# Second expert layer in seven block products instead of eight (Strassen form, chained in PSUM)

## The chip, the cores and the metric

The kernel runs on one core of one Trainium2 chip. The metric is the device time of one execution in microseconds (us); lower is better. Every kernel here was run several times beside the kernel before on the same chip. Engines are named as in the profile: PE is TensorE's matmul, PEld its weight load, DVE is VectorE, ACT is ScalarE, POOL is GpSimd.

## The reference, cut to what matters

A linear attention gives 4608 tokens of 512 values (left out). They then go through eight experts, each with two layers, whose results are weighted by a routing matrix and added.

```python
def _moe_ref(x, w_gate, w1, w2):        # x 4608 x 512, 8 experts, hidden width 1024
    ...                                 # P (4608 x 8) by eight rounds of normalising
    out = np.zeros((N, D), dtype=np.float32)
    for e in range(E):
        h = np.maximum(x @ w1[e], 0.0)  # first layer:  512 -> 1024
        ye = h @ w2[e]                  # second layer: 1024 -> 512
        out += P[:, e:e + 1] * ye
    return out.astype(np.float32)
```

## The kernel before

A small planner in the kernel (`_Plan`) takes every piece of work with its engine, an assumed duration, its dependences, its buffers and a priority, and settles the program order of each engine before anything runs. On the chip each engine works its list in that order.

The work of the experts is cut into units: one expert and one group of 512 tokens, 8 x 9 = 72 units. A unit has eight first-layer blocks (four matmuls of 512 columns each, then a relu on ScalarE that writes h in fp16) and 32 second-layer matmuls of 512 columns (four token tiles by eight pieces of the hidden width). VectorE then takes each token tile out of PSUM, the memory in which the matmuls leave their sums (this is called an eviction below), multiplies it by the routing weight and adds it to the accumulator.

```python
def unit(e, g):
    ...
    for f in range(NFT):                                   # eight first-layer blocks
        def f_hq(_, f=f, ghq=ghq, use_att=use_att):
            ...
            for c in range(NDT):
                nc.tensor.matmul(ghq["tile"], lhsT=gw1["tile"][:, c, ts(f, P)], rhs=xT[c][:, ds(512 * g, 512)],
                                 start=(c == 0), stop=(c == NDT - 1))
        def f_rl(_, ghq=ghq, gh=gh):
            gh["tile"] = hpool.tile([P, 512], FP16, tag="h", name="h")
            nc.scalar.activation(out=gh["tile"], in_=ghq["tile"], func=AF.Relu)
    ...
    for half in range(2):                                  # second layer: 2 x 4 x 4 matmuls of 512 columns
        for tt in range(4):
            def f_y(_, half=half, tt=tt):
                ...
                for f in range(4 * half, 4 * half + 4):
                    nc.tensor.matmul(gy[tt]["tile"], lhsT=hs[f]["tile"][:, ds(P * tt, P)], rhs=gw2["tile"][:, f, :],
                                     start=(f == 0), stop=(f == NFT - 1))
    ...
    for tt in range(4):                                    # eviction, experts 1 to 7
        nc.vector.scalar_tensor_tensor(out=acc[g][:, tt, :], in0=gy[tt]["tile"],
                                       scalar=P_sb[:, gg, e:e + 1], in1=acc[g][:, tt, :],
                                       op0=ALU.mult, op1=ALU.add)
```

Expert 0 is special: it runs beside the attention, before the routing weights are known, so its tiles are copied out and scaled later.

The softmax here doesn't subtract the row's maximum and nothing guards it: scores larger than these inputs give would overflow.

Of the kernel before, what the change touches and what calls it, by code (L numbers as in the profile page):

```python
# [9 lines left out]
FP32 = mybir.dt.float32  # L10
FP16 = mybir.dt.float16
# [102 lines left out]
def kernel(  # L114
# [10 lines left out]
    nc = tc.nc  # L125
# [20 lines left out]
    wpool = ctx.enter_context(tc.tile_pool(name="wpool", bufs=2))  # L146
    hpool = ctx.enter_context(tc.tile_pool(name="hpool", bufs=12))
    yps = ctx.enter_context(tc.tile_pool(name="yps", bufs=1, space=PSUM))
# [21 lines left out]
    p_vv, p_kvz, p_qpT, p_xn, p_rden = (S_.pool(2) for _ in range(5))  # L170
    p_att, p_hq, p_h = S_.pool(2), S_.pool(2), S_.pool(12)
    p_w1, p_w2 = S_.pool(2), S_.pool(2)
# [262 lines left out]
    def f_close(_):  # L435
        front.close()
        accp.append(ctx.enter_context(tc.tile_pool(name="accp", bufs=1)))
        for g in range(NA, NG):
            acc[g] = accp[0].tile([P, 4, 512], FP32, tag=f"acc{g}", name=f"acc{g}")
    t_close = add(("none", 0.0), f_close, deps=front_ids, prio=0.0)  # L440

# [4 lines left out]

    def unit(e, g):
        gw1, tw1, gw2, tw2 = w_t[e]
# [3 lines left out]
        th = []  # L452
        hs = []
        for f in range(NFT):
            use_att = e > 0 and f % 2 == 1
            ghq = S_.grp(p_att if use_att else p_hq)
            gh = S_.grp(p_h)

# [5 lines left out]

            def f_rl(_, ghq=ghq, gh=gh):
                gh["tile"] = hpool.tile([P, 512], FP16, tag="h", name="h")
                nc.scalar.activation(out=gh["tile"], in_=ghq["tile"], func=AF.Relu)  # L467
            t1 = add(("pe", 0.87), f_hq, deps=[tw1, prev_hq[0]] + xd, acq=[ghq], use=[gw1], prio=ui + 0.1 * f + 0.35)
            prev_hq[0] = t1
            th.append(add(("act", 0.6), f_rl, deps=[t1], acq=[gh], use=[ghq], prio=ui - 400.0))  # L470
            hs.append(gh)
        gy = [S_.grp(p_ye[tt]) for tt in range(4)]
        ty = [None] * 4
        for half in range(2):
            for tt in range(4):
                def f_y(_, half=half, tt=tt):
                    if half == 0:
                        gy[tt]["tile"] = yps.tile([P, 512], FP32, tag=f"ye{tt}", name=f"ye{tt}")
                    for f in range(4 * half, 4 * half + 4):
                        nc.tensor.matmul(gy[tt]["tile"], lhsT=hs[f]["tile"][:, ds(P * tt, P)], rhs=gw2["tile"][:, f, :],  # L480
                                         start=(f == 0), stop=(f == NFT - 1))
                ty[tt] = add(("pe", 0.87), f_y, deps=[tw2, ty[tt]] + th[4 * half:4 * half + 4],
                             acq=[gy[tt]] if half == 0 else [], use=[gw2] + hs[4 * half:4 * half + 4],
                             prio=ui + 0.1 * (4 * half + tt) + 0.3)
        for tt in range(4):
            gg = 4 * g + tt

            def f_fin(eng, tt=tt, gg=gg):
                if e == 0:
                    copy(eng, acc[g][:, tt, :], gy[tt]["tile"])  # L490
                else:
                    nc.vector.scalar_tensor_tensor(out=acc[g][:, tt, :], in0=gy[tt]["tile"],  # L492
                                                   scalar=P_sb[:, gg, e:e + 1], in1=acc[g][:, tt, :],
                                                   op0=ALU.mult, op1=ALU.add)
            tf = add({"act": 0.65, "dve": 0.69} if e == 0 else ("dve", 0.75), f_fin,
                     deps=[ty[tt], fin_prev.get(gg), p_done if e > 0 else None,
                           t_close if e == 0 and g >= NA else None], use=[gy[tt]], prio=ui - 400.0)
            if e == 0:
                def f_s(_, tt=tt, gg=gg):
                    nc.vector.tensor_scalar(out=acc[g][:, tt, :], in0=acc[g][:, tt, :],  # L500
                                            scalar1=P_sb[:, gg, 0:1], scalar2=None, op0=ALU.mult)
                tf = add(("dve", 0.35), f_s, deps=[tf, p_done], prio=50.0 + gg)
            fin_prev[gg] = tf
            if e == E - 1:
                def f_o(_, tt=tt, gg=gg):
                    for half in range(2):
                        bb, j = divmod(2 * gg + half, NJ)
                        dst = AP(tensor=out.tensor, offset=(S * bb + j) * DM, ap=[[NJ * DM, PW], [1, DM]])
                        nc.sync.dma_start(out=dst, in_=acc[g][64 * half:64 * half + 64, tt, :])
                add(("sp", 1.0), f_o, deps=[tf], prio=0.0)  # L510

    w_t[1] = load_w1(1, prio=0.0, after=60.0) + load_w2(1, prio=0.0, after=70.0)
    for e in range(E):
        if e >= 2:
            w_t[e] = load_w1(e, prio=float(e), deps=[w_t[e - 1][1]]) + load_w2(e, prio=float(e), deps=[w_t[e - 1][3]])
        for g in range(NG):
            unit(e, g)
    S_.run()
# [30 lines left out]
```

## Time and profile before

| | before |
|---|---|
| time, median of 4 runs | 1100.96 us |
| profiled run: span, granted TensorE clock | 1099.9 us, 0.991 |
| from the first matmul after expert 0 to the end of the last matmul's slot (its start plus the pace) | 869.65 us |
| steady unit (nine in a row take 124.32 us) | 13.813 us |
| one matmul of 512 columns, start to start (13.813 us / 64) | 215.8 ns |

In the timeline a line has the start in us, the time from the first start to the last end, the engine, the source line, the operation, what it writes and reads, the shape, how many instructions the line joins, and in brackets how long the engine had been idle and what ended that. The tile hq is a first-layer block, ye a second-layer sum in PSUM. TensorE is pipelined: the ends shown are modelled and overlap the next start. So I read its pace from starts alone. A group of eight matmuls that starts 0.87 us before the next group costs 0.87 us, even where the line says 1.04. A wait of TensorE is then the distance of two starts less the number of matmuls times their pace.

The prediction shows the steady part. The end of the kernel looks like this in the timeline before; it is needed later:

```profile
1090.18 3.89 PE L480 MATMUL ye<-w,h 128*128 128x512 f16 x16
...
1091.09 2.49 PEld L480 LDWEIGHTS <-h 128*128 128x128 f16 x13 [0.59 <-ACT h L467]
...
1093.70 0.38 PE L480 MATMUL ye<-w,h 128*128 128x512 f16 x1
```

The last unit has no next unit to put between its layers, so the last sixteen matmuls wait once for the last relu: the last of them (the third line, the end of the same group, from a narrower window) starts at 1093.70 instead of 1090.18 + 15 x 0.2158 = 1093.42, 0.28 us late, and its slot ends at 1093.91.

### The profile page before, as it was taken

The numbers are of one execution on the slowest core, as the hardware profiler recorded it, in microseconds if no ns is written. First come the engines' busy times: TensorE is split into PE (matmuls) and PEld (weight loads), VectorE is DVE, ScalarE is ACT, GpSimd is POOL, SyncE is SP. The second block draws the span as 40 slices with busy tenths as digits, with TensorE's granted clock in tenths as the row PEclk, the third lists the DMA queues.
The fourth block names the chain that finished last, engine by engine and source line by source line (L and its number), as shares of the span: only waits on it lengthen the run. The fifth ranks groups of instructions, "written<-read, shape, count | busy, mean of one in ns | idle before, by whom it ended". The sixth has DMA issues, their size and how long they took to land.

```text
span 1099.9 us, 13561 instructions
## 1 busy us (share of the span) xinstructions
PE 1060.9 (96%) x5536; PEld 504.3 (46%) x5536; DVE 355.9 (32%) x597; ACT 431.8 (39%) x693; POOL 54.8 (5%) x55
## 2 busy tenths in 40 slices
PE   3799999999999999999999999999999999999997
PEld 2455564444444444444444444444444444444443
DVE  7877866712222222222222222222222222222222
ACT  4677653443333333333333333333333333333332
POOL 3423110000000000000000000000000000000000
PEclk9799999999999999999999999999999999999999
DMA  9878400040004000040003000040003100013333
GB/s 276 320 198 249 144 1 1 1 77 1 1 1 70 8 1 1 1 77 1 1 1 63 15 1 1 1 77 1 1 1 54 24 1 1 1 39 77 77 77 77
DMA packets 31951, 55.41 MB, mean 50 GB/s; under 512 B 2704, under 2 KB 10896, under 8 KB 31888
## 3 DMA queue, kind: packets, MB, share of 16 engines
q1 hardware_dynamic: 18816, 37.76, 11.4%
q0 software_dynamic: 13072, 16.79, 9.6%
q8 instruction: 43, 0.70, 0.3%
q14 instruction: 20, 0.16, 0.0%
HBM read 61.88 MB, written 9.44 MB: 65 GB/s over the span
## 4 chain that ended last, share of the span: by engine, by line
PE 90%; DVE 6%; DMA 2%; ACT 1%; issue 0%; POOL 0%; SPq 0%; DVEq 0%; POOLq 0%; ACTq 0%
PE hq L462 44%; PE ye L480 43%; DMA vin<-in_v_dram 1%; PE kv_ps L260 1%; DMA kin<-in_k_dram 1%; DVE tk L238 1%; DVE xn L328 1%; DVE tq L238 1%; PE xt_ps L339 1%; PE qt_ps L285 1%; PE num_ps L323 0%; DVE ek L236 0%; DVE kvz L194 0%; DVE eq L236 0%; PE lg_ps L356 0%
## 5 line engine op out<-in xcount | busy, mean ns | idle before, releaser
L467 ACT ACTIVATE h<-hq 128x512 f16<-128x512 f32 x576 | 343.3, 597 | 604.5 <-PE hq L462 604.3
L462 PE MATMUL hq<-xT,w 128*128 128x512 f16 x2304 | 525.3, 379 | 0.6 <-ACT h L467 0.6
L480 PE MATMUL ye<-w,h 128*128 128x512 f16 x2304 | 525.6, 380 | 0.1
L492 DVE SCALAR_TENSOR_TENSOR acc<-ye,P_sb,acc 128x512 f32<-128x512 f32 x252 | 189.2, 751 | 679.8 <-PE ye L480 658.6
L480 PEld LDWEIGHTS <-h 128*128 128x128 f16 x2304 | 224.2, 98 | 265.9 <-issue 2.4
L462 PEld LDWEIGHTS <-w 128*128 128x128 f16 x2304 | 223.7, 98 | 263.1 <-issue 1.8
L180 POOL DMA_DIRECT2D w<-in_moe_w_dram x16 | 13.2, 828 | 694.7 <-PE hq L462 672.5
L196 POOL CAST vv<-vin 64x1152 f16<-64x1152 f32 x32 | 40.3, 1258 | 97.4 <-PE kv_ps L260 43.9
L285 PE MATMUL qt_ps<-ident,tq 128*128 128x128 f16 x144 | 13.4, 232 | 15.6 <-DVE tq L238 11.0
L260 PE MATMUL kv_ps<-vv,tk 128*128 128x260 f16 x144 | 22.1, 306 | 5.7 <-DVE qpT L194 4.1
L328 DVE TENSOR_TENSOR xn<-num_ps,rden 128x512 f16<-128x512 f32 (+1 forms) x48 | 26.5, 595 | 2.7 <-PE num_ps L323 1.9
L323 PE MATMUL num_ps<-kvz,qpT 128*128 128x128 f16 x160 | 16.2, 229 | 9.6 <-DVE xn L328 7.5
L225 ACT ACTIVATE ek<-kin 128x1152 f16<-128x1152 f32 x16 | 18.6, 1162 | 13.7 <-DMA kin<-in_k_dram 9.8
L225 ACT ACTIVATE eq<-qin 128x1152 f16<-128x1152 f32 x16 | 18.5, 1158 | 8.7 <-DVE tq L238 6.4
L192 ACT COPY acc<-ye 128x512 f32<-128x512 f32 x29 | 16.9, 584 | 10.0 <-PE ye L480 10.0
L323 PEld LDWEIGHTS <-qpT 128*128 128x128 f16 x160 | 12.3, 101 | 18.2 <-issue 12.5
L260 PEld LDWEIGHTS <-tk 128*128 128x128 f16 x144 | 14.7, 107 | 11.7 <-DVE qpT L194 4.7
L285 PEld LDWEIGHTS <-tq 128*128 128x128 f16 x144 | 10.6, 104 | 19.3 <-DVE tq L238 11.0
L238 DVE TENSOR_TENSOR tk<-tk,ek 128x1152 f16<-128x1152 f16 x16 | 17.7, 1107 | 1.1
L500 DVE TENSOR_SCALAR acc<-acc,P_sb 128x512 f32<-128x512 f32 x36 | 15.0, 490 | 9.1 <-ACT acc L192 9.1
L233 ACT ACTIVATE tk<-kin 128x1152 f16<-128x1152 f32 x11 | 12.8, 1163 | 11.1 <-PE kv_ps L260 7.1
L238 DVE TENSOR_TENSOR tq<-tq,eq 128x1152 f16<-128x1152 f16 x16 | 15.3, 959 | 1.0 <-ACT tq L233 0.2
(49 smaller groups left out, 177.1 us busy)
## 6 DMA issues: line engine op xcount, KB each, us to landing
w<-in_moe_w_dram POOLq DMA_DIRECT2D x16, 1024.0 KB, 10.7
kin<-in_k_dram SPq DMA_DIRECT2D x16, 576.0 KB, 5.5
qin<-in_q_dram SPq DMA_DIRECT2D x16, 576.0 KB, 5.0
vin<-in_v_dram SPq DMA_DIRECT2D x16, 576.0 KB, 6.3
out_dram<-acc SPq DMA_DIRECT2D x72, 128.0 KB, 2.4
wg_sb<-in_moe_w_gate_dram POOLq DMA_DIRECT2D x1, 8.0 KB, 14.8
```

Of the source, the lines that this page charges most:

```text
L192: nc.scalar.copy(out=dst, in_=src)
L196: nc.gpsimd.tensor_copy(out=dst, in_=src)
L225: nc.scalar.activation(out=ge["tile"], in_=gin[nm]["tile"], func=AF.Exp)
L238: nc.vector.tensor_tensor(out=o, in0=o, in1=ge["tile"], op=ALU.max)
L260: nc.tensor.matmul(gkv["tile"], lhsT=gt["k"]["tile"][:, j, :, :].rearrange("p r d -> p (r d)"), rhs=gvv["tile"][:, :, j, :, :], start=(j = ...
L285: nc.tensor.transpose(gp["tile"][:, j - j0, :, :].rearrange("p h w -> p (h w)"), gt["q"]["tile"][:, j, :, :].rearrange("p r d -> p (r d)") ...
L323: nc.tensor.matmul(gn["tile"][:, i - i0, :, hh, :], lhsT=gq["tile"][:, hh, js[i]:js[i] + 2, :].rearrange("p j w -> p (j w)"), rhs=gz["tile ...
L328: nc.vector.tensor_tensor(out=gxn["tile"][:, i0:i1], in0=gn["tile"][:, 0:i1 - i0].rearrange("p i r h e -> p i (r h) e"), in1=grd["tile"][: ...
L462: nc.tensor.matmul(ghq["tile"], lhsT=gw1["tile"][:, c, ts(f, P)], rhs=xT[c][:, ds(512 * g, 512)], start=(c == 0), stop=(c == NDT - 1))
L467: nc.scalar.activation(out=gh["tile"], in_=ghq["tile"], func=AF.Relu)
L480: nc.tensor.matmul(gy[tt]["tile"], lhsT=hs[f]["tile"][:, ds(P * tt, P)], rhs=gw2["tile"][:, f, :], start=(f == 0), stop=(f == NFT - 1))
L492: nc.vector.scalar_tensor_tensor(out=acc[g][:, tt, :], in0=gy[tt]["tile"], scalar=P_sb[:, gg, e:e + 1], in1=acc[g][:, tt, :], op0=ALU.mult ...
```

## The change

Two matrices cut into 2 x 2 blocks can be multiplied with seven block products instead of eight, at the cost of sums of blocks. For experts 1 to 7 the second layer does that for each pair of token tiles: the blocks A of h are 128 tokens by half of the hidden width, the blocks B of w2 are half of the hidden width by 256 output columns. Four sums S of h blocks (per unit) and four sums T of w2 blocks (per expert) are made on VectorE in fp16. The seven products m1 to m7, four matmuls of 256 columns each, are not kept apart: m1, m6, m7, m4 accumulate one after the other in the same PSUM region X, and after each of them VectorE adds the running total to the output block that needs it; m5 and m3 do the same in a region Y, and m2 stands alone in Z. The intent: an eighth of the second layer's columns less on TensorE, paid with VectorE time that lay idle.

The diff, cut to its core (h also becomes one large tile per unit instead of eight small ones, two buffers instead of twelve; expert 0 keeps the old form in `unit0`):

```diff
-    hpool = ctx.enter_context(tc.tile_pool(name="hpool", bufs=12))
+    hpool = ctx.enter_context(tc.tile_pool(name="hpool", bufs=2))
...
+    def combos(e):                       # once per expert
...
+                a0, a1, op = [(w[:, 0:4, 256:512], w[:, 0:4, 0:256], ALU.subtract),        # T1 = B12 - B11
+                              (w[:, 4:8, 256:512], T[:, 0], ALU.subtract),                 # T2 = B22 - T1
+                              (w[:, 4:8, 256:512], w[:, 0:4, 256:512], ALU.subtract),      # T3 = B22 - B12
+                              (w[:, 4:8, 0:256], T[:, 1], ALU.subtract)][i]                # T4 = B21 - T2
+                nc.vector.tensor_tensor(out=T[:, i], in0=a0, in1=a1, op=op)
...
+    def unit(e, g, gT, tT):
...
+                a0, a1, op = [(h[:, 0 + 4:8, :, 1, :], h[:, 0:4, :, 1, :], ALU.add),       # S1 = A21 + A22
+                              (Sx[:, 0], h[:, 0:4, :, 0, :], ALU.subtract),                # S2 = S1 - A11
+                              (h[:, 0:4, :, 0, :], h[:, 0:4, :, 1, :], ALU.subtract),      # S3 = A11 - A21
+                              (h[:, 4:8, :, 0, :], Sx[:, 1], ALU.subtract)][i]             # S4 = A12 - S2
+                nc.vector.tensor_tensor(out=Sx[:, i], in0=a0, in1=a1, op=op)
...
+            X, Z, Y = (gX, 0), (gX, 1), (gY, 0)
+            m1 = pm(A(1, 1), Bq(1, 1), X, True, th[0:4], True, 0.0)
+            e1 = ev(X, 0, 0, m1)
+            m5 = pm(SS(1), T(1), Y, True, [tS[0]], True, 0.1)
+            e5 = ev(Y, 1, 1, m5)
+            m2 = pm(A(1, 2), Bq(2, 1), Z, False, th[4:8] + [m1], False, 0.05)
+            ev(Z, 0, 0, m2)
+            m6 = pm(SS(2), T(2), X, False, [tS[1], e1], False, 0.2)
+            e6 = ev(X, 0, 1, m6)
+            m3 = pm(SS(4), Bq(2, 2), Y, False, [tS[3], e5], False, 0.3)
+            ev(Y, 0, 1, m3)
+            m7 = pm(SS(3), T(3), X, False, [tS[2], e6], False, 0.4)
+            e7 = ev(X, 1, 1, m7)
+            m4 = pm(A(2, 2), T(4), X, False, th[4:8] + [e7], False, 0.6)
+            ev(X, 1, 0, m4)
...
+        sub(0)                           # tiles 0 and 1 of the group
+        sub(1)                           # tiles 2 and 3
```

`pm` makes one product of four matmuls, `ev` one eviction of 256 columns with the routing weight.

More of the change, by code (lines that the diff above doesn't have):

```diff
@@ L170 @@
     p_vv, p_kvz, p_qpT, p_xn, p_rden = (S_.pool(2) for _ in range(5))
-    p_att, p_hq, p_h = S_.pool(2), S_.pool(2), S_.pool(12)
+    p_att, p_hq, p_h = S_.pool(2), S_.pool(2), S_.pool(2)
+    p_T, p_S = S_.pool(2), S_.pool(2)
     p_w1, p_w2 = S_.pool(2), S_.pool(2)
@@ L439, in f_close @@
             acc[g] = accp[0].tile([P, 4, 512], FP32, tag=f"acc{g}", name=f"acc{g}")
+        accp.append(ctx.enter_context(tc.tile_pool(name="combo", bufs=2)))
     t_close = add(("none", 0.0), f_close, deps=front_ids, prio=0.0)
@@ L445, with layer1 @@
     w_next = {}
-    def unit(e, g):
+    def layer1(e, g):
         gw1, tw1, gw2, tw2 = w_t[e]
@@ L452, in unit, with f_ha @@
         th = []
-        hs = []
+        gh = S_.grp(p_h)
+        def f_ha(_):
+            gh["tile"] = hpool.tile([P, NFT, 512], FP16, tag="h", name="h")
+        tha = add(("none", 0.0), f_ha, deps=[prev_hq[0]], acq=[gh], prio=ui - 400.0)
         for f in range(NFT):
@@ L456, in unit @@
             ghq = S_.grp(p_att if use_att else p_hq)
-            gh = S_.grp(p_h)
             def f_hq(_, f=f, ghq=ghq, use_att=use_att):
@@ L463, in f_hq, with f_rl, out_dma, f_o @@
                                      start=(c == 0), stop=(c == NDT - 1))
-            def f_rl(_, ghq=ghq, gh=gh):
-                gh["tile"] = hpool.tile([P, 512], FP16, tag="h", name="h")
-                nc.scalar.activation(out=gh["tile"], in_=ghq["tile"], func=AF.Relu)
+            def f_rl(_, f=f, ghq=ghq):
+                nc.scalar.activation(out=gh["tile"][:, f, :], in_=ghq["tile"], func=AF.Relu)
             t1 = add(("pe", 0.87), f_hq, deps=[tw1, prev_hq[0]] + xd, acq=[ghq], use=[gw1], prio=ui + 0.1 * f + 0.35)
             prev_hq[0] = t1
-            th.append(add(("act", 0.6), f_rl, deps=[t1], acq=[gh], use=[ghq], prio=ui - 400.0))
-            hs.append(gh)
+            th.append(add(("act", 0.6), f_rl, deps=[t1, tha], use=[ghq, gh], prio=ui - 400.0))
+        return gh, th
+    def out_dma(g, tt, deps):
+        def f_o(_):
+            for half in range(2):
+                bb, j = divmod(2 * (4 * g + tt) + half, NJ)
+                dst = AP(tensor=out.tensor, offset=(S * bb + j) * DM, ap=[[NJ * DM, PW], [1, DM]])
+                nc.sync.dma_start(out=dst, in_=acc[g][64 * half:64 * half + 64, tt, :])
+        add(("sp", 1.0), f_o, deps=deps, prio=0.0)
+    def unit0(g):
+        e = 0
+        gw1, tw1, gw2, tw2 = w_t[e]
+        gh, th = layer1(e, g)
         gy = [S_.grp(p_ye[tt]) for tt in range(4)]
@@ L479, in f_y @@
                     for f in range(4 * half, 4 * half + 4):
-                        nc.tensor.matmul(gy[tt]["tile"], lhsT=hs[f]["tile"][:, ds(P * tt, P)], rhs=gw2["tile"][:, f, :],
+                        nc.tensor.matmul(gy[tt]["tile"], lhsT=gh["tile"][:, f, ds(P * tt, P)], rhs=gw2["tile"][:, f, :],
                                          start=(f == 0), stop=(f == NFT - 1))
                 ty[tt] = add(("pe", 0.87), f_y, deps=[tw2, ty[tt]] + th[4 * half:4 * half + 4],
-                             acq=[gy[tt]] if half == 0 else [], use=[gw2] + hs[4 * half:4 * half + 4],
-                             prio=ui + 0.1 * (4 * half + tt) + 0.3)
+                             acq=[gy[tt]] if half == 0 else [], use=[gw2, gh],
+                             prio=g + 0.1 * (4 * half + tt) + 0.3)
@@ L485, in unit @@
         for tt in range(4):
-            gg = 4 * g + tt
-            def f_fin(eng, tt=tt, gg=gg):
-                if e == 0:
-                    copy(eng, acc[g][:, tt, :], gy[tt]["tile"])
-                else:
-                    nc.vector.scalar_tensor_tensor(out=acc[g][:, tt, :], in0=gy[tt]["tile"],
-                                                   scalar=P_sb[:, gg, e:e + 1], in1=acc[g][:, tt, :],
-                                                   op0=ALU.mult, op1=ALU.add)
-            tf = add({"act": 0.65, "dve": 0.69} if e == 0 else ("dve", 0.75), f_fin,
-                     deps=[ty[tt], fin_prev.get(gg), p_done if e > 0 else None,
-                           t_close if e == 0 and g >= NA else None], use=[gy[tt]], prio=ui - 400.0)
@@ L498, in unit, with f_fin @@
-            if e == 0:
-                def f_s(_, tt=tt, gg=gg):
-                    nc.vector.tensor_scalar(out=acc[g][:, tt, :], in0=acc[g][:, tt, :],
-                                            scalar1=P_sb[:, gg, 0:1], scalar2=None, op0=ALU.mult)
-                tf = add(("dve", 0.35), f_s, deps=[tf, p_done], prio=50.0 + gg)
-            fin_prev[gg] = tf
-            if e == E - 1:
-                def f_o(_, tt=tt, gg=gg):
-                    for half in range(2):
-                        bb, j = divmod(2 * gg + half, NJ)
-                        dst = AP(tensor=out.tensor, offset=(S * bb + j) * DM, ap=[[NJ * DM, PW], [1, DM]])
-                        nc.sync.dma_start(out=dst, in_=acc[g][64 * half:64 * half + 64, tt, :])
-                add(("sp", 1.0), f_o, deps=[tf], prio=0.0)
+            def f_fin(eng, tt=tt):
+                copy(eng, acc[g][:, tt, :], gy[tt]["tile"])
@@ new lines, in f_s @@
+            def f_s(_, tt=tt):
+                gg = 4 * g + tt
+                nc.vector.tensor_scalar(out=acc[g][:, tt, :], in0=acc[g][:, tt, :],
+                                        scalar1=P_sb[:, gg, 0:1], scalar2=None, op0=ALU.mult)
+            tf = add({"act": 0.65, "dve": 0.69}, f_fin, deps=[ty[tt], t_close if g >= NA else None],
+                     use=[gy[tt]], prio=g - 400.0)
+            tf = add(("dve", 0.35), f_s, deps=[tf, p_done], prio=NG + g - 400.0)
+            for dh in range(2):
+                fin_prev[(4 * g + tt, dh)] = tf
@@ new lines, in combos, with f_T @@
+    def combos(e):
+        gw1, tw1, gw2, tw2 = w_t[e]
+        gT = S_.grp(p_T)
+        last = None
+        for i in range(4):
+            def f_T(_, i=i):
+                if i == 0:
+                    gT["tile"] = accp[1].tile([P, 4, 4, 256], FP16, tag="T", name="T")
+                w, T = gw2["tile"], gT["tile"]
+                a0, a1, op = [(w[:, 0:4, 256:512], w[:, 0:4, 0:256], ALU.subtract),
[3 more added lines that the diff above has]
+                nc.vector.tensor_tensor(out=T[:, i], in0=a0, in1=a1, op=op)
+            last = add(("dve", 0.6), f_T, deps=[tw2, t_close, last], acq=[gT] if i == 0 else [], use=[gw2, gT],
+                       prio=NG * e - 4.0)
+        return gT, last
@@ new lines, in unit, with f_S, sub, A @@
+    def unit(e, g, gT, tT):
+        gw1, tw1, gw2, tw2 = w_t[e]
+        ui = e * NG + g
+        gh, th = layer1(e, g)
+        gS = S_.grp(p_S)
+        tS = []
+        for i in range(4):
+            def f_S(_, i=i):
+                if i == 0:
+                    gS["tile"] = accp[1].tile([P, 4, 4, 2, P], FP16, tag="S", name="S")
+                Sx = gS["tile"]
+                h = gh["tile"].rearrange("p f (s t m) -> p f s t m", s=2, t=2)
+                a0, a1, op = [(h[:, 0 + 4:8, :, 1, :], h[:, 0:4, :, 1, :], ALU.add),
[3 more added lines that the diff above has]
+                nc.vector.tensor_tensor(out=Sx[:, i], in0=a0, in1=a1, op=op)
+            tS.append(add(("dve", 0.62), f_S, deps=th + tS[-1:] + [t_close], acq=[gS] if i == 0 else [],
+                          use=[gh, gS], prio=ui - 399.0))
+        def sub(s):
+            gX, gY = S_.grp(p_ye[2 * s]), S_.grp(p_ye[2 * s + 1])
+            def A(i, j):
+                return lambda k: gh["tile"][:, 4 * (j - 1) + k, ds(256 * s + 128 * (i - 1), P)]
+            def SS(i):
+                return lambda k: gS["tile"][:, i - 1, k, s, :]
+            def Bq(i, j):
+                return lambda k: gw2["tile"][:, 4 * (i - 1) + k, ds(256 * (j - 1), 256)]
+            def T(i):
+                return lambda k: gT["tile"][:, i - 1, k, :]
+            def pm(lhs, rhs, region, first, deps, acq, prio):
+                g_, col = region
+                def f_m(_):
+                    if acq:
+                        n = 2 * s + (0 if g_ is gX else 1)
+                        g_["tile"] = yps.tile([P, 2, 256], FP32, tag=f"ye{n}", name=f"ye{n}")
+                    for kk in range(4):
+                        nc.tensor.matmul(g_["tile"][:, col, :], lhsT=lhs(kk), rhs=rhs(kk),
+                                         start=(first and kk == 0), stop=(kk == 3), skip_group_check=True)
+                return add(("pe", 0.44), f_m, deps=[tw2, tT] + deps, acq=[g_] if acq else [],
+                           use=[gw2, gT, gh, gS, g_], prio=ui + 0.3 + prio + 0.02 * s)
+            def ev(region, ti, dh, dep):
+                g_, col = region
+                gg = 4 * g + 2 * s + ti
+                def f_e(_):
+                    dst = acc[g][:, 2 * s + ti, 256 * dh:256 * dh + 256]
+                    nc.vector.scalar_tensor_tensor(out=dst, in0=g_["tile"][:, col, :], scalar=P_sb[:, gg, e:e + 1],
+                                                   in1=dst, op0=ALU.mult, op1=ALU.add)
+                t = add(("dve", 0.48), f_e, deps=[dep, fin_prev[(gg, dh)], p_done], use=[g_], prio=ui - 400.0)
+                fin_prev[(gg, dh)] = t
+                return t
+            X, Z, Y = (gX, 0), (gX, 1), (gY, 0)
[13 more added lines that the diff above has]
+            ev(X, 1, 0, m4)
+            if e == E - 1:
+                for ti in range(2):
+                    out_dma(g, 2 * s + ti, [fin_prev[(4 * g + 2 * s + ti, dh)] for dh in range(2)])
+        sub(0)
+        sub(1)
@@ L515 @@
             w_t[e] = load_w1(e, prio=float(e), deps=[w_t[e - 1][1]]) + load_w2(e, prio=float(e), deps=[w_t[e - 1][3]])
+        if e > 0:
+            gT, tT = combos(e)
         for g in range(NG):
-            unit(e, g)
+            if e == 0:
+                unit0(g)
+            else:
+                unit(e, g, gT, tT)
     S_.run()
```

## The prediction

> **What bounds the kernel now.** I read the page first: busy shares, the 40 slices and the chain that ended last.
>
> ```profile
> PE 1060.9 (96%) x5536; PEld 504.3 (46%) x5536; DVE 355.9 (32%) x597; ACT 431.8 (39%) x693; POOL 54.8 (5%) x55
> ...
> PE   3799999999999999999999999999999999999997
> DVE  7877866712222222222222222222222222222222
> ...
> PEclk9799999999999999999999999999999999999999
> ...
> PE hq L462 44%; PE ye L480 43%; DMA vin<-in_v_dram 1%; PE kv_ps L260 1%; DMA kin<-in_k_dram 1%; DVE tk L238 1%; DVE xn L328 1%; DVE tq L238 1%; PE xt_ps L339 1%; PE qt_ps L285 1%; PE num_ps L323 0%; DVE ek L236 0%; DVE kvz L194 0%; DVE eq L236 0%; PE lg_ps L356 0%
> ```
>
> From the eighth slice on TensorE is full at full clock, VectorE is at two tenths, and 87% of the chain is the two expert layers. Busy is not proof of speed, so I took the order of time in one steady stretch, all engines.
>
> ```profile
> 600.68 3.62 PE L480 MATMUL ye<-w,h 128*128 128x512 f16 x16
> 603.91 3.33 PEld L462 LDWEIGHTS <-w 128*128 128x128 f16 x16
> 604.13 3.62 PE L462 MATMUL hq<-xT,w 128*128 128x512 f16 x16
> 605.25 0.60 ACT L467 ACTIVATE h<-hq 128x512 f16<-128x512 f32 x1 [3.72 <-PE hq L462]
> ...
> 607.58 3.62 PE L480 MATMUL ye<-w,h 128*128 128x512 f16 x16
> ...
> 608.65 3.34 DVE L492 SCALAR_TENSOR_TENSOR acc<-ye,P_sb,acc 128x512 f32<-128x512 f32 x4 [10.47 <-PE ye L480]
> ```
>
> Sixteen matmuls start every 3.45 us, 215.6 ns each, with nothing between the groups. One unit (512 tokens, one expert) is 32 + 32 of them, 13.81 us; the sixteen weight loads of the second row lie under the matmuls. So the time falls by what TensorE has less to stream, unless something new makes it wait. There are 8 x 9 = 72 units; the change touches experts 1 to 7, 63 units.
>
> **What the Trainium skill says.** (1) "TensorE: Matmul & The Clock Gate", Back-to-back issue gap: warm spacing is N/2.4 + 2.5 ns, so 216 at 512 columns and 109 at 256. The trace agrees at 512 (215.6). The same section's "sustained" figure of 131 ns at 512 is not what this trace shows. (2) The same page, step 1 of "Step-by-step: what each phase is for": the next weights load while the current matmul runs. The question is whether a load still fits under a matmul half as long. The front of this kernel has the answer: nine matmuls of 260 columns, each with its own weights.
>
> ```profile
> 50.95 1.16 PE L260 MATMUL kv_ps<-vv,tk 128*128 128x260 f16 x9
> 51.84 0.42 PEld L300 LDWEIGHTS <-qpT 128*128 128x128 f16 x10
> 51.95 0.40 PE L300 MATMUL den_ps<-kvz,qpT 128*128 128x2 f16 x10
> ...
> 57.13 0.72 PE L339 MATMUL xt_ps<-ident,xn 128*128 128x128 f16 x10
> 57.64 0.58 PEld L462 LDWEIGHTS <-w 128*128 128x128 f16 x4
> 57.69 1.03 PE L462 MATMUL hq<-xT,w 128*128 128x512 f16 x4
> ```
>
> The nine take 51.95 - 50.95 = 1.00 us, 111 ns each; ten of 128 columns take 0.56 us, 56 ns each. So a load costs at most 56 ns and hides under 256 columns. Between 260 and 512 columns the slope is (215.6 - 111.1)/252 = 0.415 ns a column, so 256 columns take 109.4 ns. (3) "VectorE: DVE Perf Modes", The perf-mode tier table: tensor_tensor on 16-bit SBUF data runs two elements a cycle, with any PSUM or fp32 operand one. The trace agrees.
>
> ```profile
> L492 DVE SCALAR_TENSOR_TENSOR acc<-ye,P_sb,acc 128x512 f32<-128x512 f32 x252 | 189.2, 751 | 679.8 <-PE ye L480 658.6
> ...
> 113.66 0.44 DVE L236 TENSOR_SCALAR ek<-ek 128x1152 f16<-128x1152 f16 x1
> 114.20 0.76 DVE L238 TENSOR_TENSOR tk<-tk,ek 128x1152 f16<-128x1152 f16 x1
> ```
>
> 1152 fp16 elements in 0.76 us (the minimum and the median of that line are 757 to 759 ns; the 1.6 us ones lie beside GpSimd casts, and GpSimd casts nothing in the expert part) is 600 ns of streaming at 1.92 elements a ns plus 157; so 1024 elements take 533 + 157 = 690 ns. The eviction of 512 fp32 is 533 + 218 = 751; of 256 it is 267 + 218 = 485 ns. (4) "PSUM — Partial Sum Buffer", PSUM bank collisions raise a hardware error: two engines must not touch one bank and quadrant at once. The change puts two products (columns 0 and 256) in one bank, so a product must wait for the eviction of its neighbour; the built order has such waits (m2 waits for the eviction after m1). No run yet shows what they cost.
>
> **The change part by part.**
>
> TensorE, removed: 32 matmuls of 512 columns per unit, 32 x 215.6 = 6.90 us. Added: two halves x seven products x four = 56 matmuls of 256 columns, 56 x 109.4 = 6.13 us. Gain 0.77 us a unit, 63 x 0.773 = 48.7 us. (7/8 of 6.90 would be 6.04; the 24 additional issues take back 0.09.)
>
> VectorE per unit, removed: 4 x 751 = 3.0 us. Added: 14 evictions x 485 = 6.8 and four sums of h x 690 = 2.8, together 9.55 us in a unit of 13.81 - 0.77 = 13.04 us, 73%. It fits in throughput. Per expert four weight sums more, 2.8 us.
>
> What matters is latency, since the products chain: m1, m6, m7, m4 accumulate in one region with an eviction between each, and m5, m6, m3, m7 need the h sums. I built the changed kernel and read its order. TensorE's steady unit is: m1, f6, f7, f0', m2, m5, f1', f2', m6, f3', m3, m7, f4', m4, f5', where m stands for both halves (0.875 us), f for one first-layer block (0.862), and a prime is the next unit's. VectorE's is: E1 E1, S1, E2 E2, E5 E5, S2, S3, S4, E6 E6, E3 E3, E7 E7, E4 E4.
>
> Latencies from the trace: PE to ACT 0.26 us after the slot's end (604.13 + 0.86 to 605.25), relu 0.60, PE to DVE 0.20 (the group of four from 607.58 ends at 608.44, eviction at 608.65), and DVE to PE about 0.06 (with 0.06 more where a weight load comes first).
>
> *Tightest place, m5.* f7's slot ends at 0; relu done 0.86; S1 from 0.90 to 1.59; weights and matmul at 1.71. TensorE has f0' and m2 to do, 0.862 + 0.875 = 1.74. It fits by 0.03 us.
> *m6.* Let m5 start at T = 0. S1 ended at -0.12; E2, E2, E5, E5 follow (about 0.40 apart when nothing holds them, the second E5 at 1.1 after its product), S2 from about 1.5 to 2.2, m6 possible at 2.32; TensorE has m5, f1', f2' = 2.60. Slack 0.28.
> *m3, m7, m4, next m1.* m3 needs S4 (3.4) at 4.3; m7 needs E6 (3.8) at 5.2; m4 needs E7 (6.3) at 6.9; m1' needs E4 (8.05) at 8.7. Slack 0.5 us or more each.
>
> So on paper nothing stalls. I put in 0.03 us a unit for the two tight places, 2 us.
>
> *Weight sums.* For expert 1 they stand before the routing iteration, where VectorE is idle for 3.6 us and w2 came long before; 2.85 fit. For the others they stand in the first unit of the expert before, between evictions, and wait for w2. Their place is 12 us or more after the matmuls that free the buffer, and the load lands in 10.7 us (median). Slack 1.6 us at the tightest (expert 2). Nothing to 2 us in all; I take 0.5.
>
> *Front.* TensorE's built order is the same up to the end of expert 0. No change.
>
> *Tail.* The last unit has no next unit to fill the chain. By the same ladder, from its m1 at 0: S1 done 4.2, m5 4.3, S2 done 6.5, m6 6.6, m3 7.8, m7 8.7, m4 9.9 to 10.8 against 7.8 us without waits; the last tiles come at 11.0 and 11.5, and four output transfers are then still to be issued (0.59 us each, last issue to landing 2.4). Before, the same queue limited the end. I get 2.5 us more.
>
> Sum: 1101.6 - 48.7 + 2.0 + 0.5 + 2.5 = 1057.9; I take 1057.
>
> **The rivals.**
>
> *A stall at m5 or m6 in every unit.* For it: 0.03 us of slack, and a chain in program order with no way around. A stall of 0.3 us a unit would take 19 us: 1076. If the sums ran at one element a cycle (1.22 us), m5 would wait 0.5 us and m6 more, so 1090 or worse. Against: the strided tk sum has the same kind of access (runs of 64) and reaches 757 ns.
>
> *Weight loads become the bound at 256 columns.* If each pair took 125 ns, the 56 would take 7.0 us and the gain is gone: about 1108. Against: 111 ns at 260 columns and 56 ns at 128 are in the trace.
>
> *VectorE becomes the bound.* It needs 9.55 of 13.04 us; it would have to be 37% slower than worked out. Evictions that collide with the sums of the next expert could cost 1 to 2 us for each of six experts: 1065.
>
> *A late w2 holds VectorE's queue in the first unit of each expert.* 25.3 us is the longest landing in the trace, but in the busy front. If each came 3 us late: 1072.
>
> **Range and chances.** Most errors point upwards (stalls), few down (the tail, the taken 2 us). Range 1050 to 1070. Faster by over 2% means below 1079.5; that fails only if a stall of 0.35 us sits in every unit. Faster 0.91, within 2% 0.08, slower 0.01.
>
> **What would show it.** In the profile after: 56 matmuls of 256 columns per unit, with groups of eight starting 0.87 us apart; a unit of 13.0 to 13.1 us; VectorE at seven tenths; evictions of about 485 ns and sums of about 690; TensorE idle before S-fed products near zero except in the last unit; the chain still on PE. I am wrong if idle time "<- DVE S" or "<- DVE acc" sums to over 10 us, if a 256-column matmul takes more than 115 ns, or if the front differs.

## The result, and the profile after

| | before | after |
|---|---|---|
| median (lowest to highest), 4 runs each | 1100.96 us (1100.27 to 1102.07) | 1053.85 us (1052.90 to 1055.08) |
| profiled span | 1099.9 us | 1053.3 us |
| first matmul after expert 0 to end of the last matmul's slot | 869.65 us | 822.10 us |
| steady unit | 13.813 us | 13.02 us |

The ratio is 0.9572, with a 95% interval of 0.9555 to 0.9588. Ratios here are the mean time of one kernel's fast runs over that of the other's of the same rounds, so they are not quite the ratio of the medians quoted. All outputs are right.

The page of the kernel after, busy shares, VectorE's 40 slices and the chain that ended last:

```profile
PE 1012.7 (96%) x7048; PEld 652.9 (62%) x7048; DVE 730.2 (69%) x1507; ACT 432.1 (41%) x693; POOL 54.8 (5%) x55
...
DVE  6787876847666766667666766677666766666666
...
PE 88%; DVE 7%; DMA 2%; ACT 1%; issue 1%; POOL 0%; SPq 0%; DVEq 0%; POOLq 0%; ACTq 0%
```

VectorE went from two to six or seven tenths, and from 355.9 to 730.2 us of work. PE is still at 96%, and it is 88% of the chain (90% before). VectorE's share of the chain is 7% (6% before), so nearly all of the 374 us of new VectorE work are off the path. The costliest groups of the same page (busy us and mean ns, then the idle time before them):

```profile
L587 DVE SCALAR_TENSOR_TENSOR acc<-ye,P_sb,acc 128x256 f32<-128x256 f32 x882 | 396.7, 483 | 144.4 <-PE ye L576 144.4
...
L576 PE MATMUL ye<-T,S 128*128 128x256 f16 x1512 | 196.0, 273 | 1.2 <-DVE S L550 1.2
...
L550 DVE TENSOR_TENSOR S<-h 128x1024 f16<-128x1024 f16 x126 | 86.8, 689 | 115.4 <-ACT h L471 115.4
```

An eviction lasts 483 ns and a sum 689. VectorE waits 115 us for h before the first sum of each unit. In the whole program, the matmuls fed by T and S were held up for 1.2 us in the profile's count. A steady unit at its narrowest place, in order of time, all engines (ScalarE left out):

```profile
608.06 2.75 PE L467 MATMUL hq<-xT,w 128*128 128x512 f16 x12
...
610.62 0.69 DVE L550 TENSOR_TENSOR S<-h 128x1024 f16<-128x1024 f16 x1 [1.87 <-ACT h L471]
610.65 1.04 PE L576 MATMUL ye<-w,h 128*128 128x256 f16 x8
...
611.42 0.86 PEld L576 LDWEIGHTS <-S 128*128 128x128 f16 x8
611.53 1.04 PE L576 MATMUL ye<-T,S 128*128 128x256 f16 x8
...
613.00 0.68 DVE L550 TENSOR_TENSOR S<-S,h 128x1024 f16<-128x1024 f16 x1
...
613.91 0.97 PEld L576 LDWEIGHTS <-S 128*128 128x128 f16 x8
614.13 1.04 PE L576 MATMUL ye<-T,S 128*128 128x256 f16 x8
```

The sum S1 starts at 610.62, once the relu of the block before is done, and ends at 611.31. The twelve first-layer matmuls in front of m2 keep the pace of the kernel before (610.65 - 608.06 = 2.59 us, 215.8 ns each). The weights of m5, which are S1, are loaded at 611.42, and m5 starts at 611.53, which is 610.65 + 0.88: the pace of eight matmuls, no wait. S2 ends at 613.68, and m6's weights follow at 613.91. No wait there either. Unlike this, the last unit, TensorE alone:

```profile
1039.45 0.49 PE L576 MATMUL ye<-w,h 128*128 128x256 f16 x3
1040.30 0.72 PE L576 MATMUL ye<-w,h 128*128 128x256 f16 x5 [0.36 <-ACT h L471]
1041.03 1.05 PE L576 MATMUL ye<-T,S 128*128 128x256 f16 x8
1043.25 1.05 PE L576 MATMUL ye<-T,S 128*128 128x256 f16 x8 [1.18 <-DVE S L550]
1044.46 1.05 PE L576 MATMUL ye<-w,S 128*128 128x256 f16 x8 [0.16 <-DVE S L550]
1045.34 1.04 PE L576 MATMUL ye<-T,S 128*128 128x256 f16 x8
1046.52 1.03 PE L576 MATMUL ye<-T,h 128*128 128x256 f16 x8
```

Eight matmuls take 8 x 0.1092 = 0.87 us. The starts are later than that by 0.52 (the second half of m2 waits for h), 0.18 (m5), 1.35 (m6), 0.34 (m3) and 0.31 us (m4): together 2.7 us. Here each link of the chain shows, since no first-layer block lies between.

The balance closes. The 63 changed units save 63 x (13.813 - 13.02) = 49.96 us; the last unit gives back 2.7 - 0.28 (the wait that was there before) = 2.42. That leaves 47.54, and the expert part became 869.65 - 822.10 = 47.55 us shorter. In these two profiled executions the part before the first matmul after expert 0 was 1.03 us longer after (225.29 against 224.26 us), and what follows the last matmul 0.12 shorter, which makes the 46.6 us between the spans. The first of these is no effect of the change that the runs can tell: in another execution of the kernel after (the last run below) that part took 223.23 us.

### The profile page after: what moved, and what is told of

The parts are those of the page before. It is cut to its first block, busy times and chain, and to the rows that moved or that the text cites. A ratio compares the mean times of both kernels' runs of the same rounds, so it can differ in the third digit from the quotient of the medians.

```text
span 1053.3 us, 17028 instructions
## 1 busy us (share of the span) xinstructions
PE 1012.7 (96%) x7048; PEld 652.9 (62%) x7048; DVE 730.2 (69%) x1507; ACT 432.1 (41%) x693; POOL 54.8 (5%) x55
## 4 chain that ended last, share of the span: by engine, by line
PE 88%; DVE 7%; DMA 2%; ACT 1%; issue 1%; POOL 0%; SPq 0%; DVEq 0%; POOLq 0%; ACTq 0%
PE hq L467 45%; PE ye L576 36%; PE ye L497 4%; DMA vin<-in_v_dram 1%; DMA kin<-in_k_dram 1%; PE kv_ps L261 1%; DVE tk L239 1%; DVE xn L329 1%; DVE tq L239 1%; PE xt_ps L340 1%; PE qt_ps L286 1%; PE num_ps L324 0%; DVE ek L237 0%; DVE gs L389 0%; DVE kvz L195 0%
## 5 line engine op out<-in xcount | busy, mean ns | idle before, releaser
L587 DVE SCALAR_TENSOR_TENSOR acc<-ye,P_sb,acc 128x256 f32<-128x256 f32 x882 | 396.7, 483 | 144.4 <-PE ye L576 144.4
L576 PEld LDWEIGHTS <-S 128*128 128x128 f16 x2016 | 197.0, 98 | 51.4 <-DVE S L550 2.2
L576 PE MATMUL ye<-T,S 128*128 128x256 f16 x1512 | 196.0, 273 | 1.2 <-DVE S L550 1.2
L576 PEld LDWEIGHTS <-h 128*128 128x128 f16 x1512 | 147.9, 98 | 58.1 <-ACT h L471 0.6
L550 DVE TENSOR_TENSOR S<-h 128x1024 f16<-128x1024 f16 x126 | 86.8, 689 | 115.4 <-ACT h L471 115.4
L576 PE MATMUL ye<-w,h 128*128 128x256 f16 x1008 | 130.8, 273 | 0.4 <-ACT h L471 0.4
L497 PE MATMUL ye<-w,h 128*128 128x512 f16 x288 | 69.7, 385 | 0.0
L576 PE MATMUL ye<-w,S 128*128 128x256 f16 x504 | 65.3, 273 | 0.2 <-DVE S L550 0.2
L576 PE MATMUL ye<-T,h 128*128 128x256 f16 x504 | 65.3, 273 | 0.1
L497 PEld LDWEIGHTS <-h 128*128 128x128 f16 x288 | 27.1, 100 | 27.5 <-issue 2.2
L550 DVE TENSOR_TENSOR S<-h,S 128x1024 f16<-128x1024 f16 x63 | 43.2, 686 | 0.0
```

The lines of the kernel that those rows point to most:

```text
L497: nc.tensor.matmul(gy[tt]["tile"], lhsT=gh["tile"][:, f, ds(P * tt, P)], rhs=gw2["tile"][:, f, :], start=(f == 0), stop=(f == NFT - 1))
L550: nc.vector.tensor_tensor(out=Sx[:, i], in0=a0, in1=a1, op=op)
L576: nc.tensor.matmul(g_["tile"][:, col, :], lhsT=lhs(kk), rhs=rhs(kk), start=(first and kk == 0), stop=(kk == 3), skip_group_check=True)
L587: nc.vector.scalar_tensor_tensor(out=dst, in0=g_["tile"][:, col, :], scalar=P_sb[:, gg, e:e + 1], in1=dst, op0=ALU.mult, op1=ALU.add)
```

## The experiments

The theory (A): TensorE's stream is the bound before and after, the gain is the saved columns alone, and VectorE's work is hidden because each piece has its place in the order, with small known slacks at m5 and m6. The rivals: the rest of the change helped too; loads at 256 columns have a price; or VectorE simply had room, and the order does not matter.

### Everything of the change but the products

All experts use the old form, with the new h tiles and priorities (the diff is cut: the sums of w2 go as well, and `unit0` gets the old eviction for experts 1 to 7).

```diff
-            if e == 0:
-                unit0(g)
-            else:
-                unit(e, g, gT, tT)
+            unit0(g, e)          # eight products for every expert; experts 1 to 7 evicted as before
```

> All experts by the eight products of before, but with everything else of the change kept (h in two large tiles, the new priorities); its TensorE order is that of before over the whole program. Theory A (the whole gain is the TensorE columns that the seven products save): as before, 1101 us, between 1098 and 1104. Rival (part of the gain comes from the rest of the change): below 1090 us.

Measured: 1100.28 us, beside 1100.49 of the kernel before; ratio 0.9998 (0.9982 to 1.0015). The whole gain comes from the second layer's new form; the large h tiles neither cost nor bring anything.

### Eight products in matmuls of 256 columns

```diff
+                        for dh in range(2 if e > 0 else 1):
+                            w = 256 if e > 0 else 512
-                        nc.tensor.matmul(gy[tt]["tile"], lhsT=..., rhs=gw2["tile"][:, f, :], ...)
+                            nc.tensor.matmul(gy[tt]["tile"][:, ds(256 * dh, w)], lhsT=...,
+                                             rhs=gw2["tile"][:, f, ds(256 * dh, w)], ...)
```

> As the run above, but in experts 1 to 7 every second-layer matmul of 512 columns is two of 256, so that the weights are loaded twice as often, as in the changed kernel, with no product saved. Theory A (a matmul of 256 columns costs half of one of 512 plus about 2.6 ns, and the weight load stays hidden): 63 units x (64 x 109.2 - 32 x 215.8 ns) = 5 us above the run above, 1106 us. Rival (weight loads that come every 256 columns set a floor, say 125 ns): 63 x 64 x 16 ns = 65 us above it.

Measured: 1107.39 us (ratio to before 1.0058, 1.0043 to 1.0073), 7.1 us above the run without the split. Its steady stretch, TensorE and its loads:

```profile
603.00 3.59 PEld L499 LDWEIGHTS <-h 128*128 128x128 f16 x32
603.22 3.66 PE L499 MATMUL ye<-w,h 128*128 128x256 f16 x32
...
606.71 3.62 PE L467 MATMUL hq<-xT,w 128*128 128x512 f16 x16
```

Thirty-two matmuls with 32 loads take 606.71 - 603.22 = 3.49 us, 109.1 ns each. Seven half units take 48.63 us (603.22 to 651.85), so a unit takes 13.894 us, 0.081 more than before, and 63 of them make the 5 us expected. The other 2 us are not in the units. In the profiled executions the part from the first matmul after expert 0 to the end of the last slot is 5.0 us longer than in the run without the split (874.62 against 869.59), and the part before it, which the edit leaves as it was, 1.9 us longer (224.65 against 222.78). That part differs as much between two executions of the kernel after (225.29 and 223.23). Why all four runs with the split lie close together (1107.05 to 1107.61), while those without go from 1100.15 to 1101.77, stays open. The rival with a floor of 125 ns, 65 us, is out: 256 columns are enough to hide a load of a full 128 x 128 block.

### The first sum made twice

```diff
-                nc.vector.tensor_tensor(out=Sx[:, i], in0=a0, in1=a1, op=op)
+                for _r in range(2 if i == 0 else 1):
+                    nc.vector.tensor_tensor(out=Sx[:, i], in0=a0, in1=a1, op=op)
```

> The changed kernel with the first activation sum S1 made twice in each unit, with the same TensorE order. Theory A (VectorE is hidden by its place in the order, and S1 is the one sum without slack: it waits for ScalarE's last h and m5 waits for it): the second copy of 0.69 us comes straight on the path, less the few hundredths of slack: 63 x 0.66 = 41 us, 1095 us. Rival (there are seconds of VectorE idle in each unit, so 0.69 us more of it is hidden anywhere): 1054 us.

Measured: 1090.75 us, 36.9 above the kernel after, 0.586 us a unit. The mechanism holds and the size is a tenth smaller. The same place of the timeline, VectorE and the loads:

```profile
612.08 1.42 DVE L551 TENSOR_TENSOR S<-h 128x1024 f16<-128x1024 f16 x2 [1.25 <-ACT h L471]
...
613.41 1.71 DVE L588 SCALAR_TENSOR_TENSOR acc<-ye,P_sb,acc 128x256 f32<-128x256 f32 x4
...
613.55 0.77 PEld L577 LDWEIGHTS <-S 128*128 128x128 f16 x8 [0.68 <-DVE S L551]
```

The two copies take 1.42 instead of 0.69 us, so the second one adds 0.73 (it writes the same tile, and it starts at 612.80, after the first has ended at 612.77). Its end at 613.50 releases the load at 613.55, and the matmuls start with the load. In the kernel after, the load stood 0.11 us ahead of its matmul. So the slack at m5 was 0.73 - 0.586 = 0.14 us: about 0.06 before the load would have had to wait (0.05 after 611.31, against 611.42), and the load's lead of about 0.1.

### The same work in another place

An instruction of the same shape goes to a scratch tile right after the pair of evictions after m1, where VectorE waits for h.

```diff
                     nc.vector.scalar_tensor_tensor(out=dst, ...)
+                    if s == 1 and region is X and (ti, dh) == (0, 0):
+                        w = gw2["tile"]
+                        scr = accp[1].tile([P, 4, 256], FP16, tag="scr", name="scr", bufs=1)
+                        nc.vector.tensor_tensor(out=scr, in0=w[:, 0:4, 256:512], in1=w[:, 0:4, 0:256], op=ALU.subtract)
```

> The changed kernel with one more sum of the same size as S1 on VectorE in each unit, but right after the pair E1, in the 1.87 us gap in which VectorE waits for h before S1. Theory A (place decides, not the load): 1054 us, between 1052 and 1057. Rival (what more work on VectorE costs depends on its sum): the same cost as when S1 is made twice, about 1095 us.

Measured: 1053.03 us, ratio 0.9565 (0.9550 to 0.9579) against 0.9572 of the kernel after: no cost. In the timeline the added sum takes part of the gap, and S1 stays where it was:

```profile
606.50 0.68 DVE L592 TENSOR_TENSOR scr<-w 128x1024 f16<-128x1024 f16 x1
608.45 0.69 DVE L550 TENSOR_TENSOR S<-h 128x1024 f16<-128x1024 f16 x1 [1.27 <-ACT h L471]
```

VectorE is busy for 768.4 us in this run and 764.6 in the run with S1 twice, and yet this one is 37.7 us faster. Place decides, not the load.

### The second sum made twice

The same edit as for the first sum, with `i == 1`.

> The changed kernel with the second activation sum S2 made twice in each unit, with the same TensorE order. Theory A (the slack at m6 is about 0.23 us): 63 x (0.69 - 0.23) = 29 us, 1083 us, less than S1 twice. Rival (all of VectorE's work behind S1 is on the path, as S1 ends with no slack): 63 x 0.69 = 43 us, the same as or more than S1 twice.

Measured: 1076.06 us, 22.2 above the kernel after, 0.352 us a unit; less than for S1, as the theory has it, and less than the 29 us expected. The timeline again has the reason:

```profile
607.74 1.41 DVE L551 TENSOR_TENSOR S<-S,h 128x1024 f16<-128x1024 f16 x2
...
609.20 0.77 PEld L577 LDWEIGHTS <-S 128*128 128x128 f16 x8 [0.67 <-DVE S L551]
```

The second copy adds 1.41 - 0.68 = 0.73 us, and the slack at m6 was 0.73 - 0.352 = 0.38 us, where I had put 0.23. In the kernel after, the load could have started at 613.68 + 0.05 = 613.73 and started at 613.91 (0.18 us), and it stood 0.22 us ahead of its matmul. Together that is 0.40. So both expectations left out the load's lead on its matmul: a late load uses up this lead before TensorE stands still.

### No overlap between units

The first layer of a unit waits, in the plan, for the last product of the unit before. The work is the same, only the order differs.

```diff
+    last_m4 = [None]
-            t1 = add(("pe", 0.87), f_hq, deps=[tw1, prev_hq[0]] + xd, ...)
+            t1 = add(("pe", 0.87), f_hq, deps=[tw1, prev_hq[0], last_m4[0]] + xd, ...)
...
+            last_m4[0] = m4
```

> The changed kernel with each unit's first layer held behind the last product of the unit before, so that no first-layer block lies between the products. Theory A (the interleaved first-layer blocks are what hides ScalarE's h, the sums and the evictions; the last unit, which has none, waited about 2.0 us): 61 units more with about 2.0 us each, 1177 us, slower than before. Rival (VectorE has room, so the order of the blocks matters little): 1054 to 1065 us.

Measured: 1220.44 us, ratio 1.1090 (1.1071 to 1.1108): 166.6 us above the kernel after, slower than the kernel before by 120. The direction is the theory's; the size was off, since I had read the last unit's wait as about 2.0 us, from the brackets. Read from the starts it is 2.7 us (above), and 62 units more with 2.7 us make 167. Two lines of one unit of this run, TensorE alone:

```profile
705.64 1.05 PE L578 MATMUL ye<-T,S 128*128 128x256 f16 x8 [1.18 <-DVE S L552]
706.84 1.05 PE L578 MATMUL ye<-w,S 128*128 128x256 f16 x8 [0.16 <-DVE S L552]
```

The first line is m6: it waits for S2, which stands behind four evictions in VectorE's order, and the second is m3, which waits for S4; in each unit, as in the last one of the kernel after. So seven products alone would have lost: the interleaved first-layer blocks are what pays for the chain.

### The last unit in the old form

```diff
-            if e == 0:
-                unit0(g)
+            if e == 0 or (e == E - 1 and g == NG - 1):
+                unit0(g, e)
```

> The changed kernel with the last unit alone (last expert, last group) by the eight products of before. Theory A (the last unit has no first layer beside it and waits about 2.0 us for h and the sums, against 0.79 us that seven products save): 1.2 us less, about 1052.6 us. Rival (the wait for the last h is there in either form, so only the products count): 0.8 us more, about 1054.7 us.

Measured: 1052.06 us over six runs, ratio 0.9555 (0.9542 to 0.9568). That is 1.8 us below the kernel after, but the intervals overlap. The traces tell more: from the start of S1 in the unit before to the end of the span, it is 24.4 us here (1026.79 to 1051.2) and 26.0 in the kernel after (1027.26 to 1053.3), 1.6 us less. By the corrected tail one expects 2.7 - 0.28 - 0.79 = 1.6.

### Expert 0's last groups in the new form too, and the kernel after once more

Expert 0 finds VectorE busy with the attention and the routing. Only its last two groups have their second layer after the routing weights are done, so only they can be evicted with them. The diff is shown against the run before, so the last unit keeps the old form here too.

```diff
+            if e == 0 and g >= NA:                       # NA = 7; two groups
+                ...  nc.gpsimd.memset(acc[g], 0.0)  ...   # the evictions add to it
-            if e == 0 or (e == E - 1 and g == NG - 1):
+            if (e == 0 and g < NA) or (e == E - 1 and g == NG - 1):
                 unit0(g, e)
             else:
                 unit(e, g, gT, tT)
```

> The changed kernel with the last unit by eight products, as in an earlier run (1052.06 us, 0.9555 of before), and the last two groups of expert 0, whose second layer comes after the routing weights are known, by seven products too (their output tiles are set to zero first, on GpSimd). Theory A (a unit by seven products is 0.79 us shorter wherever VectorE has room): 2 x 0.79 = 1.6 us less than that run, about 1050.5 us, ratio about 0.954. Rival (next to the routing iteration and the scaling of the tiles VectorE has no room): the sums come late, the units stall, 1052 us or more.

> The changed kernel itself once more, unedited, on the same chip as the run beside it, so that differences of one or two us can be read. Expected 1053.8 us; theory A: 3 us above the run with expert 0's last groups by seven products; rival: the same as it.

Measured, on the same chip: 1051.10 us (1050.24 to 1051.82; ratio 0.9548, 0.9535 to 0.9562) against 1053.03 us (1052.73 to 1054.65; ratio 0.9568, 0.9555 to 0.9581) for the kernel after, unedited. The medians differ by 1.9 us where 3 were expected; the intervals of the ratios just overlap. In the profiled runs of both, the last step of the routing weights starts at the same time (200.43 and 200.37 us), the same point in expert 1 comes 1.2 us earlier (1.6 expected), and the spans differ by 2.7 (1048.5 and 1051.2). The profile of this run names no wait of TensorE for a sum in the whole program. So there was room for these two groups, and this is the fastest of the kernels, though by an amount close to what the runs can resolve.

## Why the prediction was right

It was right in its direction, its mechanism and its range: 1053.85 us lie inside 1050 to 1070, 3.2 below the 1057 given. Several sizes were off, nearly all to the same side. By its steps:

**TensorE.** It had 0.773 us a unit from 215.6 and 109.4 ns a matmul. The unit fell from 13.813 to 13.02, 0.793: the paces are 215.8 ns and, from (13.02 - 32 x 0.2158) / 56, 109.2 ns. The term was undersized by 63 x 0.02 = 1.3 us. The run with the old form and the rest of the change (ratio 0.9998) shows that nothing else contributed, and the run with 256 columns that the added loads are hidden.

**Weight loads as the bound.** This rival rested on what it would cost if a pair took 125 ns. It takes 109. The argument from the 260-column matmuls of the front was the right one.

**VectorE.** Its rates were right: 483 ns an eviction (485 predicted), 689 a sum (690). Its load was a little lower: in the steady unit from 605.00 to 618.02 it is busy for 8.70 us, 67%, where 9.55 us and 73% were worked out, because an eviction or sum can start while the one before it has not ended (in the lines of the run with S1 twice, four evictions of 0.48 us take 1.71 us). The bank rule of its point (4) cost nothing: the evictions after m1 end at 608.75, and m2 starts at 610.65.

**Two tight places.** The ladder named m5 and m6 as the narrow ones, in this order, and the doubled sums show it (36.9 and 22.2 us), while the same work elsewhere is free. The slacks were undersized: 0.03 and 0.28 us on paper, 0.14 and 0.38 measured. The traces show two parts of that. The sums end earlier: S1 1.52 us after f7's slot (611.31 against 610.65 - 0.86 = 609.79), where the ladder has 1.59, and S2 2.15 us after m5's start, where it has 2.2. And the ladder has 0.12 us from a sum's end to its matmul, half of that for a weight load that comes first; a late load and its matmul start together, 0.06 us after the sum (613.50 to 613.55 in the run with S1 twice). Together that makes 0.16 and 0.39 us. So the 2.0 us put in for stalls were not there. This is the largest of the terms that were off.

**Weight sums.** 0.5 us were put in; no wait of TensorE for T shows in the trace. From one unit's first m1 to the next one's it is 13.02 us for 61 of the 62 steps, those with weight sums among them; the first step is longer by one first-layer block (13.88 us), which the order has in front there. So in experts 1 to 7 neither the weight sums nor a late w2 cost anything. I made no run on this alone.

**Front.** It said no change. Up to the first matmul after expert 0 it is 224.26 us before and 225.29 and 223.23 us in the two profiled executions after: no difference that these can tell.

**Tail.** It had 2.5 us more; the starts give 2.7 us of waits against 0.28 before, 2.4 more. Its ladder's own chain was a little longer, 10.8 - 7.8 = 3.0 us of waits, of which it kept 2.5 with a look at the output transfers; but from the end of the last matmul's slot to the end of the span it is 5.9 to 6.0 us in both kernels, so all of it is in the chain of products.

Put together with the measured terms: 1100.96 - 49.96 + 2.42 = 1053.4 us against 1053.85 measured. The prediction's sum was 1057.9 us, 4.5 more: 2.0 for stalls, 1.3 for the columns, 0.5 for the weight sums, 0.1 in the tail, and 0.6 because it started from 1101.6 us instead of 1100.96. The remaining 0.5 us is less than the distance between two runs of the same kernel. One reading of its first lines was wrong without consequence: VectorE's row falls to one or two tenths from the ninth slice on, not the eighth, which is still a 7.

## What to carry to other kernels

When one engine's stream is the bound, as here, a rewrite that trades its work for that of an idle engine gains what the stream loses if each new piece gets a place in the order with slack before its reader: 0.69 us of VectorE work cost nothing in one place of the unit and 0.59 us in another. Keep independent work of the bound engine (here the next unit's first layer) between the links of a dependent chain, and use the old form where there is none, as at the end of the program (1.6 us by the traces, though the run times do not resolve it). Read waits of a pipelined engine from distances of starts, and count the lead of a weight load as slack.

## What the Trainium skill lacked or had wrong

- "TensorE: Matmul & The Clock Gate", Back-to-back issue gap: its "sustained" 131 ns at 512 columns and 81 ns at 128, for a stream of load and matmul pairs, are shown by no run here. Pairs take 215.8 ns at 512 columns and 109.2 at 256 (109.1 in the run with eight products), and 56 ns at 128 in the front. The formula that the section calls isolated, N/2.4 + 2.5, is the one that holds in the stream.
- The same page, "The mechanism" (what overlaps and what doesn't): it says that a load overlaps with running matmuls only when the row groups differ, against the page's own step 1 of "Step-by-step: what each phase is for". Here loads of full 128 x 128 blocks lie under matmuls of full 128 x 128 blocks, 64 second-layer loads a unit without a cost beyond the matmuls' own pace (13.894 us a unit, 0.081 more than with 32; 64 x 109.2 - 32 x 215.8 ns makes 0.083).
- The same page does not say how far a load runs ahead of its matmul. In these traces it is one matmul of the stream: 0.11 us where the matmul before has 256 columns (m5 in the steady unit), 0.22 where it has 512 (m6). It counts as slack where the weights come late: it is a part of the 0.14 us at m5 and of the 0.38 at m6.
- "VectorE: DVE Perf Modes", The TRN2 errata: its table gives 120 + FD cycles at 0.96 GHz for an operand in PSUM, 392 ns at 256 elements. A single eviction lasts 483 ns (751 at 512, table 658); but in a row where nothing holds them they start (1.71 - 0.48) / 3 = 0.41 us apart. So, taken for the duration that a reader on another engine waits for, the row is about 92 ns short, and it is nearer to the distance of starts. The section's own check finds its SBUF figure short of a single operation's duration, and does not check the PSUM one. For a sum of 1024 fp16 elements the table's 58 + 512 cycles are 594 ns; these start 0.60 us apart and last 0.69.
- No page that I found gives the time from one engine's end to the next one's start for these pairs. Here it is about 0.26 us from a matmul's slot to ScalarE, 0.20 from a matmul's slot to VectorE, and 0.05 from VectorE's end to TensorE's weight load.
